# Reordering the start of a two-layer linear-attention and gated-MLP kernel: loads on one queue, LayerNorm on GpSimd, query weights transposed by DMA

## The chip, the cores and the metric

The kernel runs on one core of a Trainium2 chip. The metric is device time in microseconds (us) of one execution, median of several runs. The core's engines work side by side: TensorE (PE in the profile; PEld is its weight load), VectorE (DVE), ScalarE (ACT), GpSimd (POOL) and SyncE (SP), which here only issues DMAs. ScalarE can issue DMAs too.

## The reference

All tensors are bf16; S = 2048 tokens, D = 576 columns, H = 32 heads of 18 columns, F = 4608. Two layers, each an attention part A and a gated part B with the same weights in both layers:

```python
def _A_ref(x, wqkv, w_phi, wo):
    q, k, v = heads(x @ wqkv)
    pq = einsum("bhsd,hdf->bhsf", q, w_phi);  pk = einsum("bhsd,hdf->bhsf", k, w_phi)
    phi_q = concat([softmax(pq), softmax(-pq)]);  phi_k = concat([softmax(pk), softmax(-pk)])
    kv = einsum("bhsf,bhsd->bhfd", phi_k, v);  z = phi_k summed over s
    o = einsum("bhqf,bhfd->bhqd", phi_q, kv) / (einsum("bhqf,bhf->bhq", phi_q, z) + 1e-6)
    return merged(o) @ wo
def _B_ref(x, w_gate, w_up, w_down):
    return ((x @ w_gate) * (x @ w_up)) @ w_down

x = x + _A_ref(_layernorm(x), ...)
x = x + _B_ref(_layernorm(x), ...)
x = x + _A_ref(_layernorm(x), ...)
x = x + _B_ref(_layernorm(x), ...)
```

The LayerNorm has no weights. The attention is linear: `kv` and `z` need all tokens of the layer before any token's output can be formed.

## The kernel before

**Tiles.** The tokens are 16 tiles of 128, handled in 8 pairs. x stays in SBUF (`x_sb`). For each tile, LayerNorm statistics are made on VectorE (L1111, L1119), the logarithm and exponential that give 1/sqrt(variance) on ScalarE (L1132, L1134), and the normalised tile `xln` is written by one TENSOR_SCALAR (L1144). `xln` has 640 columns: its last 64 of 576 are repeated behind them, so that the two halves of TensorE's rows both have them after the transpose into `xT`. The transpose is TensorE's with a copy (L1152, L1155, the `fast` argument of `t_ln`, used where latency counts) or a DMA transpose issued by SP (L1159). For the plain pairs, `t_ln` writes 576 and 64 columns of each tile in two operations, both on GpSimd, or, for layer 1's attention (`boot`), both on GpSimd or VectorE as the planner prefers.

**Stages.** First come the loads (`t_load`: raw q and k weights `Wraw` in five slabs, x tiles, v weights), a test on the weights that writes `flag` (`t_flag`, L931 to L944), and the fusion of `w_phi` into the k and q weights (`t_fuse1`: a transpose of a slab into `WTk` or `WTq`, L1057 and L1060, then matmuls with a block-diagonal `BDphi`, L1071, and a cast, L1076). After the flag the program branches: with these inputs the branch without maxima (`fast=True`) runs. There, each tile gets a k and a v projection (L1185), four exponentials (`dd`, L1306), their sums (L1373, VectorE), reciprocals (L1376 on VectorE or L1380 on ScalarE), two products with them (L1388, GpSimd; VectorE for the last two tiles) and its key-value matmuls (L1427). When all 16 are through, `t_barrier` forms `BD` (L1518), tiles 0 and 1 are finished by `t_aout` (L1575 to L1639), normalised, and the gated part starts: L1715 (gate and up), L1762 and L1764 (product), L1789 and L1791 (down), pair by pair. The query projections of tiles 2 to 15 (`t_qproj`, L1330) fill TensorE meanwhile. Layer 1's gated part is interleaved with layer 2's key-value work (`k2`, `t_kv`) and with the attention outputs of later tiles. In `t_aout`, for tiles from 2 on, the last 64 columns of the attention output are repeated too, by a VectorE copy, before a DMA transpose.

**Memory that is shared in time.** `Wraw` and `WTk`, `WTq` lie where `Wg` and `Wu` (gate and up weights) are loaded later. So the last four of the eight loads of `Wg` and `Wu` wait for the fused q weights, and the first four for the last pair's `xT`.

**Order.** The program is written by a planner (`Sched`) when it is built. Each piece of work is a generator that yields operations with an estimated duration, the tiles read and written, and events. At each step the planner takes the waiting operation with the smallest key, its estimated start less several terms:

```python
key = (est - self.bias.get(int(th.prio), 0.0) - th.age - th.age0 - (self.hold if late else th.boost), -th.prio)
```

`age0` comes from the table `AGES` at the top of the file, in nanoseconds by the generator's name. An `alt` request names several engines and the planner takes the one that it expects to finish first. An operation with `port=True` on VectorE is planned not to overlap one on GpSimd. Every engine and queue then runs its list strictly in the planned order, with semaphore waits where a tile is produced elsewhere. Parameters in `K.__init__` steer the generators: `sload` and `aload` (early loads of SP's and ScalarE's queue), `lnb` (from which pair LayerNorm waits for the branch), `lnlead` and `vlead` (how far LayerNorm and v run ahead of key-value work), `qlead` (when the first query tiles start), `pqg` (when query projections may start), `fqp`, `fage2` (priorities), `wtdma` (which weights are transposed by DMA).

Of the kernel before, what the change touches and what calls it, by code (L numbers as in the profile page):

```python
# [8 lines left out]
ALU = mybir.AluOpType  # L9
# [7 lines left out]


AGES = {
    "ain1_0": 96, "ain1_1": 52, "ain1_11": -60, "ain1_12": -492, "ain1_13": 86, "ain1_14": -147, "ain1_5": -137, "ain1_6": -193, "ain1_9": -273,  # L20
    "ain2_14": -438, "ain2_15": -340, "aout1_0": -130, "aout1_1": -102, "aout1_2": -169, "aout1_3": -149, "aout2_0": -365, "aout2_1": 28,
    "aout2_2": -170, "aout2_3": -392, "bar1": -205, "bar2": 31, "bdphi": 104, "bepi0": -915, "bepi6": 256, "bepi7": -330, "flag": -70, "fusek0": -120,
    "fusek1": -40, "fusek2": 301, "fusek3": -147, "fuseq0": -35, "fuseq1": -124, "fuseq2": -148, "fuseq3": -151, "init": 401, "k2_6": -418,
    "k2ln0": 766, "k2ln1": 1415, "kv2_7": -134, "lnA1_0a": 245, "lnA1_0b": 360, "lnA1_2": 62, "lnA1_3": 52, "lnA1_4": -54, "lnB1_0a": -675,
    "lnB1_0b": -631, "lnB2_0a": -815, "lnB2_0b": -579, "pq1_10": -131, "pq1_11": 213, "pq1_2": 262, "pq1_3": -196, "pq1_4": -111, "pq1_5": 12,
    "pq1_6": 145, "pq1_9": 334, "pq2_11": 118, "pq2_12": 428, "pq2_15": 112, "pq2_2": 322, "pq2_3": 281, "pq2_4": 41, "pq2_5": 296, "pq2_6": -35,
    "pq2_8": -91, "v1_0": 39, "v1_1": -420, "v1_11": -111, "v1_13": -244, "v1_15": 580, "v1_2": -281, "v1_3": -122, "v1_5": -127, "v1_6": -124,
    "v1_8": -122, "v2_14": -755, "v2_15": -878,
}


# [265 lines left out]
class Sched:  # L297
# [110 lines left out]
    def run(self):  # L408
        tr = self.tr
        while True:  # L410
# [83 lines left out]
            for th in self.threads:  # L494
# [10 lines left out]
                elif r[0] == "pe2":  # L505
                    ops = r[1 + self.pe_mode]
                    est = max(self.free_at["pe"], self.ready(th, 10 + self.pe_mode, "pe", ops, True), th.t_ready)
                    th.alt = ("ops", "pe", ops, self.pe_mode)
                elif r[0] == "ops":
                    eng = r[1]  # L510
# [17 lines left out]
            if r[0] == "ops":  # L528
                eng = r[1]
                t = est  # L530
                first = True
                t_beg = t
                for o in r[2]:
                    deps = tr.deps_for(eng, o.reads, o.writes, o.excl, True, o.order)
                    if not first:
                        t = max(t, tr.ready_time(deps, eng))
                    if eng == "pe" and o.mode != self.pe_mode:
                        self.pe_mode = o.mode
                        if not first:
                            t += self.pe_switch  # L540
                    first = False
                    fin = t + o.dur
                    tr.record(eng, o.emit, o.reads, o.writes, o.excl, fin, deps)
                    self.busy[eng] += o.dur
                    t = fin
                    if eng == "pool" or o.port:
                        self.port[eng] = fin
                if self.log is not None:
                    self.log.append((th.name, eng, t_beg, t, len(r[2]), self.free_at[eng]))
                self.free_at[eng] = t  # L550
            else:
                _, group, emit, reads, writes, nbytes, dram_write = r[:7]
                immediate = r[7] if len(r) > 7 else False
                issue = est
                queue = r[9] if len(r) > 9 else "sp"
                if hasattr(self, "mark_time"):
                    start = max(issue, self.dma_free["sp"])
                    xfer = nbytes / self.dma_bw
                else:
                    start = max(issue + 1250.0, self.dma_free["sp"])  # L560
                    left, u = nbytes, start
                    for end, rate in ((3400.0, 290.0), (5000.0, 150.0), (1e9, 335.0)):
                        if u < end and left > 0:
                            d_ = min(left / rate, end - u)
                            left, u = left - d_ * rate, u + d_
                    xfer = u - start
                self.dma_free["sp"] = start + xfer
                sp_time = r[8] if len(r) > 8 else 480.0
                fin = max(start + xfer + (self.dma_lat if hasattr(self, "mark_time") else 600.0), issue + 2.1 * sp_time) + (1500.0 if sp_time > 1000 else 0.0)
                tr.record_dma(group, emit, reads, writes, fin, queue, dram_write, immediate)  # L570
                self.free_at[queue] = issue + sp_time
# [5 lines left out]
S, D, FF, H, DH = 2048, 576, 4608, 32, 18  # L577
# [58 lines left out]
class K:  # L636
    def __init__(self, nc, A_x, A_wqkv, A_w_phi, A_wo, B_w_gate, B_w_up, B_w_down, out, fast, base=None):
# [7 lines left out]
        self.XPS, self.XSM, self.XVX, self.NMX = (0, 6, 9, 0) if fast else (1, 4, 9, 2)  # L645
        self.BOUND = 40.0
        self.vrow = True
        self.vlead = 5
        self.row2 = True
        self.wtdma = ''  # L650
        self.valt = False
        self.qalt = True
        self.sload = [['x0', 0], ['raw', 0], ['x0', 1], ['raw', 2], ['raw', 3], ['raw', 4], ['wv', 0], ['x', 3]]
        self.aload = [['raw', 1], ['x', 1], ['x', 2]]
        self.rord = (0, 1, 2, 3, 4)
        self.fage = 300
        self.fageq = 0.0
        self.fage2 = 300
        self.lnb = 3
        self.pes = (0, 1, 2, 3, 4, 5, 6, 7, 8, 9, 10, 11, 12, 13)  # L660
        self.early = (2, 2)
        self.pex = 2
        self.qlead = 12 if fast else 8
        self.alt = 1.2
        self.wage = 10
        self.lnage = -3
        self.lnlead = 8
        self.pol0 = 1
        self.qdeep = (1, 1)
        self.urgent = 4  # L670
        self.pqp = (3, 3)
        self.pqg = 8 if fast else 10
        self.NPQ = 3
        self.NLAST = 3
        self.pqd = 100
# [1 line left out]
        self.qcrit = False  # L677
        self.fq = 3
        self.fqs = 2
        self.fqp = 6.5 if fast else 6.5  # L680
        self.sub2pool = False
        self.rboost = 500.0
        self.prio0 = (6, 7)
# [238 lines left out]
    def t_flag(self):  # L922
        s = self
        yield ("wait", "init")
        yield ("age", s.fage2)
        for kt in range(5):
            yield ("wait", ("ld", "raw", s.rord[kt]))
            if kt == 0:
                gots = yield ("acqn", ["pb"], 2)
                banks = [g_[1] for g_ in gots]  # L930
            yield ("ops", "pe", [Op(55, (lambda e, m=m, c0=c0, kt=s.rord[kt], bank=banks[m // 3], c=128 * (m % 3), st=(kt == 0 and c0 == 0 and m in (0, 3)), sp=(kt == 4 and c0 > 0): e.matmul(  # L931
                s.ps[:, bank, c:c + 128], s.Wraw[:, kt, c0 + 128 * m:c0 + 128 * m + 128], s.Wraw[:, kt, c0 + 128 * m:c0 + 128 * m + 128], start=st, stop=sp, skip_group_check=True)),
                reads=[("Wraw", s.rord[kt])], writes=[("pbd", banks[m // 3])], excl=[("pb", banks[m // 3])]) for c0 in (0, D) for m in range(5)])
        yield ("ops", "dve", [Op(d_dve(n), (lambda e, c=c, bank=bank, n=n: e.tensor_reduce(s.cst[:, c:c + 1], s.ps[:, bank, 0:n], AX.X, ALU.max)),
                                 reads=[("pbd", bank)], writes=[("cst", c)], excl=[("pb", bank)]) for c, bank, n in ((1, banks[0], 384), (2, banks[1], 256))])

# [150 lines left out]
    def t_ln(self, tiles, sig, fast=False, slot=None, banks=None):  # L1087
        s = self
# [47 lines left out]
        for j in js:  # L1136
# [4 lines left out]
                                                        bias=s.nmr[:, sl[j]:sl[j] + 1], scale=rstd[:, sl[j]:sl[j] + 1])),  # L1141
                      reads=xr + [("nmr", sl[j]), ("rstd", sl[j])], writes=[("xln", sl[j])]),
                   Op(240, (lambda e, j=j: e.copy(xln[:, sl[j], 576:640], xln[:, sl[j], 512:576])), reads=[("xln", sl[j])], writes=[("xln", sl[j])])]
            em = [(lambda e, j=j, a=a, b=b, c=c: e.tensor_scalar(xln[:, sl[j], a:b], x_sb[:, ss[j], c:c + b - a], s.nmean[:, sl[j]:sl[j] + 1], rstd[:, sl[j]:sl[j] + 1],  # L1144
                                                                 ALU.add, ALU.mult)) for a, b, c in ((0, 576, 0), (576, 640, 512))[:2 - fast]]
            yield ("alt", [(eng, [Op(d, em[i], reads=[("x", ss[j], 0), ("x", ss[j], 1), ("nmean", sl[j]), ("rstd", sl[j])], writes=[("xln", sl[j])], port=eng == "dve") for i, d in enumerate(dur)])
                           for eng, dur in (("pool", (790, 370)[:2 - fast]), ("dve", (400,) if fast else (400, 215)))[:1 + (fast or boot)]])
        for j in js:
            if fast:
                (_, bank), = yield ("acqn", ["pb"], 1)  # L1150
# [208 lines left out]
    def softmax_tail(self, sm, crit, pz=None, exps=True):  # L1359
# [25 lines left out]
        for br in range(2):  # L1385
            ev = dd[:, sm, :, br, :]
            rb = ss[:, sm, :].rearrange("p (g b) -> p g b", b=2)[:, :, br].unsqueeze(2).to_broadcast([128, H, DH])
            yield ("alt", [(eng, [Op(dur, (lambda e, ev=ev, rb=rb: e.tensor_tensor(ev, ev, rb, ALU.mult)),  # L1388
                                     reads=s.ddk(sm, br) + [("ss", sm)], writes=s.ddk(sm, br))])
                           for eng, dur in ((("pool", 1150), ("dve", 675))[crit > 1:1 + (crit > 1)] if s.fast else (("pool", 1150), ("dve", 675))[:1 + (crit > 1)])])  # L1390

    def t_v(self, L, st_):
# [134 lines left out]
    def t_aout(self, L, st_):  # L1527
# [69 lines left out]
            ops.append(Op(d_dve(288), (lambda e, i=i, ov=ov, rb=rb: e.tensor_tensor(ov, nv[i][:, :, 0:DH], rb, ALU.mult)),  # L1597
                          reads=[("pbd", banks[i])] + denk, writes=[okeys[i]] + okeys[2:], excl=[("pb", banks[i])]))
        if st_ >= 2:
            ops.append(Op(130, (lambda e: e.tensor_copy(o[:, 576:640], o[:, 512:576])), reads=okeys, writes=okeys))  # L1600
        yield ("ops", "dve", ops)
        yield ("rel", "o", ob)
        for bank in banks:
            yield ("rel", "pb", bank)
# [475 lines left out]
```

## Time and profile before

| | us |
|---|---|
| median of 9 runs | 1076.73 |
| lowest, highest | 1074.65, 1080.02 |
| the profiled execution's own time | 1076.34 |
| its span, first to last instruction | 1074.6 |
| first gated-unit matmul of layer 1 (L1715) | 101.9 |
| first gated-unit matmul of layer 2 | 619.5 |

How to read the profile: "L1144" is a line of the kernel; a group row gives the line, engine, operation, `out<-in` tiles and shapes, the count, then busy us and mean ns of one, then the engine's idle time before it and what ended it. "SPq" and "ACTq" are DMA issues. A busy PE is one with matmuls in its pipeline, not one at full rate. The granted TensorE clock was 0.998 of full speed over the span.

### The profile page before, as it was taken

How to read it: one execution, taken by the hardware profiler on the slowest of the kernel's cores; microseconds unless marked ns; L12 is line 12 of the kernel's file. 1: busy time of each engine (PE TensorE's matmuls, PEld its weight loads, DVE VectorE, ACT ScalarE, POOL GpSimd, SP SyncE). 2: the span in 40 equal slices, each digit the busy share in tenths (PEclk: the TensorE clock that was granted, in tenths of full speed). 3: DMA queues.
4: the chain of work that ended last, by engine and by line, in shares of the span. 5: the costliest groups of instructions: out<-in, count | busy, mean ns of one | idle time of the engine just before them, and what ended most of it. 6: DMA issues, size and time to landing. Idle time of an engine off the chain costs nothing.

```text
span 1074.6 us, 34340 instructions
## 1 busy us (share of the span) xinstructions
PE 1051.1 (98%) x15766; PEld 804.2 (75%) x15828; DVE 484.0 (45%) x982; ACT 346.6 (32%) x839; POOL 196.2 (18%) x226
## 2 busy tenths in 40 slices
PE   7989999999999999999999999999999999999997
PEld 5657868778686878878686786777778686868683
DVE  6976526354443535425232754434434243424131
ACT  5777214324141422314141742231313131302030
POOL 2753004022230403103020030201010101000000
PEclk9999999999999999999999999999999999999999
DMA  5496265260927246182605134636282808081704
GB/s 168 85 292 209 42 180 93 80 168 21 226 28 201 60 117 140 35 195 37 199 15 167 34 59 122 137 86 173 60 199 36 222 16 241 16 223 15 210 2 146
DMA packets 177626, 127.79 MB, mean 119 GB/s; under 512 B 96576, under 2 KB 175680, under 8 KB 176320
## 3 DMA queue, kind: packets, MB, share of 16 engines
q1 hardware_dynamic: 176176, 124.57, 45.2%
q8 instruction: 126, 2.06, 0.8%
q10 hardware_dynamic: 1296, 0.92, 0.3%
q14 instruction: 28, 0.23, 0.1%
HBM read 100.82 MB, written 2.36 MB: 96 GB/s over the span
## 4 chain that ended last, share of the span: by engine, by line
PE 92%; DVE 2%; DMA 2%; ACT 2%; issue 1%
PE ps L1715 53%; PE ps L1789 20%; PE ps L1185 11%; PE ps L1791 4%; PE ps L1575 1%; DVE xln L1144 1%; DVE ss_w4f L1373 1%; DMA wdr<-in_B_w_down_dram 1%; DMA wdx<-in_B_w_down_dram 1%; PE ps L1427 1%; ACT dd_h1g L1306 1%; PE ps L1173 0%; PE ps L1152 0%; DMA wst<-in_A_w_phi_dram 0%; ACT dd_w3f L1306 0%
## 5 line engine op out<-in xcount | busy, mean ns | idle before, releaser
L1715 PE MATMUL ps<-xT,Wg 64*128 64x256 bf16 x4608 | 581.9, 269 | 0.0
L1715 PE MATMUL ps<-xT,Wu 64*128 64x256 bf16 x4608 | 581.1, 269 | 0.0
L1715 PEld LDWEIGHTS ps<-xT,Wg 64*128 64x128 bf16 x4608 | 430.6, 94 | 29.1 <-issue 3.1
L1715 PEld LDWEIGHTS ps<-xT,Wu 64*128 64x128 bf16 x4608 | 431.8, 94 | 27.3
L1764 DVE TENSOR_TENSOR hT<-ps,hT 128x512 bf16<-128x512 f32 x288 | 199.1, 691 | 303.9 <-ACT hT L1762 303.9
L1762 ACT CAST hT<-ps 128x512 bf16<-128x512 f32 x288 | 168.4, 585 | 413.6 <-PE ps L1715 406.6
L1789 PE MATMUL ps<-wdr,hT 128*128 128x512 bf16 x922 | 237.9, 380 | 0.7 <-DMA wdr<-in_B_w_down_dram 0.6
L1388 POOL TENSOR_TENSOR dd<-dd,ss 128x576 bf16<-128x576 bf16 x92 | 106.6, 1185 | 490.2 <-ACT ss L1384 490.1
L1791 PE MATMUL ps<-wdr,hT 128*128 128x64 bf16 x960 | 184.9, 193 | 2.3 <-issue 0.5
L1789 PEld LDWEIGHTS ps<-wdr,hT 128*128 128x128 bf16 x960 | 93.8, 98 | 112.0 <-DMA wdr<-in_B_w_down_dram 1.6
L1715 PE MATMUL ps<-xT,Wr 64*128 64x256 bf16 x1152 | 168.3, 269 | 0.0
L1832 DVE TENSOR_TENSOR x_sb<-ps,x_sb 128x64 bf16<-128x64 f32 x32 | 7.0, 219 | 225.8 <-PE ps L1791 225.8
L1144 POOL TENSOR_SCALAR xln<-x_sb,nmean,rstd 128x576 bf16<-128x576 bf16 x86 | 51.7, 607 | 254.4 <-DVE nmean L1125 173.6
L1791 PEld LDWEIGHTS ps<-wdr,hT 128*128 128x128 bf16 x960 | 94.1, 98 | 0.2
L1384 ACT ACTIVATE ss<-ss 128x64 f32<-128x64 f32 x92 | 23.5, 258 | 178.6 <-DVE ss L1373 177.7
L1373 DVE TENSOR_REDUCE ss<-dd 128x64 f32<-128x1152 bf16 x48 | 63.5, 1345 | 20.0 <-ACT dd L1306 18.9
L1715 PEld LDWEIGHTS ps<-xT,Wr 64*128 64x128 bf16 x1152 | 65.1, 94 | 6.3
L1185 PE MATMUL ps<-Wk,xT 64*128 64x288 bf16 x576 | 49.0, 284 | 2.8 <-ACT Wq L1076 1.7
L1185 PE MATMUL ps<-Wv,xT 64*128 64x288 bf16 x576 | 49.8, 283 | 1.6 <-ACT eT L1551 0.5
L1789 PE MATMUL ps<-wdx,hT 128*128 128x512 bf16 x168 | 50.4, 380 | 0.4 <-DMA wdx<-in_B_w_down_dram 0.3
L1111 DVE BATCH_NORM_STATS2 st<-x_sb 128x6 f32<-128x288 bf16 x120 | 46.2, 444 | 1.4 <-DMA x_sb<-in_A_x_dram 1.3
L1185 PE MATMUL ps<-Wq,xT 64*128 64x288 bf16 x576 | 41.1, 283 | 0.6 <-ACT dd_w3f L1306 0.4
(125 smaller groups left out, 740.9 us busy)
## 6 DMA issues: line engine op xcount, KB each, us to landing
wdr<-in_B_w_down_dram SPq DMA_DIRECT2D x240, 288.0 KB, 3.5
wdx<-in_B_w_down_dram SPq DMA_DIRECT2D x48, 288.0 KB, 3.5
Wg<-in_B_w_gate_dram SPq DMA_DIRECT2D x4, 1152.0 KB, 13.8
Wu<-in_B_w_up_dram SPq DMA_DIRECT2D x4, 1152.0 KB, 15.6
out_dram<-x_sb SPq DMA_DIRECT2D x16, 144.0 KB, 2.5
x_sb<-in_A_x_dram SPq DMA_DIRECT2D x5, 288.0 KB, 3.7
Wraw<-in_A_wqkv_dram SPq DMA_DIRECT2D x4, 304.0 KB, 6.2
xT<-xln SPq DMA_TRANSPOSE x54, 2.5
```

Of the source, the lines that this page charges most:

```text
L1111: ops.append(Op(d_dve(288), (lambda e, j=j, h=h, src=src: e.bn_stats(st[:, sl[j], 6 * h:6 * h + 6], src)), reads=rd, writes=[("st", sl[j], ...
L1144: em = [(lambda e, j=j, a=a, b=b, c=c: e.tensor_scalar(xln[:, sl[j], a:b], x_sb[:, ss[j], c:c + b - a], s.nmean[:, sl[j]:sl[j] + 1], rstd[ ...
L1185: out.append(Op(61, (lambda e, h=h, k=k, st=(i == 0 and k == 0), sp=(i == 1 and k == 3): e.matmul(s.ps[:, banks[h], 0:N], L[r, k, :], Wm[r ...
L1306: yield ("ops", "act", [Op(d_actc(288), (lambda e, br=br, h=h, bank=bank: e.activation(s.dd[:, sm, 16 * h:16 * h + 16, br, :], s.ps[:, ban ...
L1373: Op(1265, (lambda e: e.tensor_reduce(ss[:, sm, :], e4, AX.X, ALU.add)), reads=s.ddk(sm, 0) + s.ddk(sm, 1), writes=[("ss", sm)]),
L1384: yield ("ops", "act", [Op(200, (lambda e, kw=kw: e.activation(ss[:, sm, :], ss[:, sm, :], **kw)), reads=[("ss", sm)], writes=[("ss", sm)])])
L1388: yield ("alt", [(eng, [Op(dur, (lambda e, ev=ev, rb=rb: e.tensor_tensor(ev, ev, rb, ALU.mult)), reads=s.ddk(sm, br) + [("ss", sm)], write ...
L1715: out.append(Op(54.3, (lambda e, bank=bank, cs=cs, lhsT=lhsT, rhs=rhs, st=st, sp=sp: e.matmul(ps[:, bank, cs].rearrange("p (a n) -> p a n" ...
L1762: yield ("ops", "act", [Op(480, (lambda e, gb=gb, p=p: e.copy(hT[:, p, :], ps[:, gb, :])), reads=[("gu", gb)], writes=[("hT", p)] + (s.raw ...
L1764: yield ("ops", "dve", [Op(600, (lambda e, ub=ub, p=p: e.tensor_tensor(hT[:, p, :], ps[:, ub, :], hT[:, p, :], ALU.mult)), reads=[("gu", u ...
L1789: ops = [Op(d_pe(512), (lambda e: e.matmul(s.ps[:, bank, 0:512], lhsT, s.wslot(slot)[:, fi, 0:512], start=(f == 0), stop=(f == NF - 1))), ...
L1791: Op(d_pe(64) + 3, (lambda e: e.matmul(s.ps[:, z, 64 * sl:64 * sl + 64], lhsT, s.wslot(slot)[:, fi, 512:576], start=(f == 0 and (sl == 0 o ...
```

## The change

- `AGES` is replaced by another table, and these parameters get other values: `vlead` 5 to 7, `lnb` 3 to 5, `lnlead` 8 to 7, `qlead` 12 to 14, `pqg` 8 to 10, `fqp` 6.5 to 6.15, `fage2` 300 to 600 (all for the branch that runs, or both). The planner's estimate of the early DMA rate is 350 instead of 335 bytes per ns.
- All early loads but `w_phi` go to SP's queue, raw weight slabs 1 and 2 first; `t_flag` takes the slabs in the order of loading.
- The q weights are transposed by DMA from SP (`wtdma = 'q'`), not by TensorE with a copy.
- Plain pairs are normalised on GpSimd alone (`lndve = False`), one operation of 576 columns for each tile, and the repeat of the last 64 columns is one operation for both tiles, on GpSimd or ScalarE.
- The VectorE alternative of the softmax products is marked `port`; the repeat of the attention output's last columns is planned as an operation of its own, marked `port`.

```diff
@@ Sched.run
-                    for end, rate in ((3400.0, 290.0), (5000.0, 150.0), (1e9, 335.0)):
+                    for end, rate in ((3400.0, 290.0), (5000.0, 150.0), (1e9, 350.0)):
@@ K.__init__
-        self.vlead = 5
+        self.vlead = 7
-        self.wtdma = ''
+        self.lndve = False
+        self.wtdma = 'q'
-        self.sload = [['x0', 0], ['raw', 0], ['x0', 1], ['raw', 2], ['raw', 3], ['raw', 4], ['wv', 0], ['x', 3]]
-        self.aload = [['raw', 1], ['x', 1], ['x', 2]]
-        self.rord = (0, 1, 2, 3, 4)
+        self.sload = [['raw', 1], ['raw', 2], ['x0', 0], ['x0', 1], ['raw', 3], ['raw', 0], ['raw', 4], ['wv', 0], ['x', 1], ['x', 2], ['x', 3]]
+        self.aload = []
-        self.fage2 = 300
-        self.lnb = 3
+        self.fage2 = 600
+        self.lnb = 5
-        self.qlead = 12 if fast else 8
+        self.qlead = 14 if fast else 8
-        self.lnlead = 8
+        self.lnlead = 7
-        self.pqg = 8 if fast else 10
+        self.pqg = 10 if fast else 10
-        self.fqp = 6.5 if fast else 6.5
+        self.fqp = 6.15 if fast else 6.5
@@ t_flag
+        rord = [k_[1] for k_ in s.sload if k_[0] == "raw"]
...
@@ t_ln
-            em = [(lambda e, j=j, a=a, b=b, c=c: e.tensor_scalar(xln[:, sl[j], a:b], x_sb[:, ss[j], c:c + b - a], s.nmean[:, sl[j]:sl[j] + 1], rstd[:, sl[j]:sl[j] + 1],
-                                                                 ALU.add, ALU.mult)) for a, b, c in ((0, 576, 0), (576, 640, 512))[:2 - fast]]
...
+            em = (lambda e, j=j: e.tensor_scalar(xln[:, sl[j], 0:576], x_sb[:, ss[j], :], s.nmean[:, sl[j]:sl[j] + 1], rstd[:, sl[j]:sl[j] + 1], ALU.add, ALU.mult))
...
+                           for eng, dur in (("pool", 790), ("dve", 400))[:1 + (fast or (boot and s.lndve))]])
+        if not fast:
+            xo, xi = xln[:, s0:s1, 576:640], xln[:, s0:s1, 512:576]
+            yield ("alt", [(eng, [Op(dur, em, reads=key("xln"), writes=key("xln"))]) for eng, dur, em in (
+                ("pool", 420, lambda e: e.tensor_copy(xo, xi)), ("act", 210, lambda e: e.copy(xo, xi)))])
@@ softmax_tail
-                                     reads=s.ddk(sm, br) + [("ss", sm)], writes=s.ddk(sm, br))])
+                                     reads=s.ddk(sm, br) + [("ss", sm)], writes=s.ddk(sm, br), port=eng == "dve")])
@@ t_aout
-            ops.append(Op(130, (lambda e: e.tensor_copy(o[:, 576:640], o[:, 512:576])), reads=okeys, writes=okeys))
-        yield ("ops", "dve", ops)
+            ops.append(Op(100, (lambda e: e.tensor_copy(o[:, 576:640], o[:, 512:576])), reads=okeys, writes=okeys, port=True))
+        yield ("ops", "dve", ops[:2])
+        if st_ >= 2:
+            yield ("ops", "dve", ops[2:])
```

## The prediction

> **What bounds the kernel now.** I read the page first. TensorE is busy nearly all of the span, the other engines less than half of it.
>
> ```profile
> PE 1051.1 (98%) x15766; PEld 804.2 (75%) x15828; DVE 484.0 (45%) x982; ACT 346.6 (32%) x839; POOL 196.2 (18%) x226
> ```
>
> That average hides stages, so the second view is the windows table, cut where the timeline shows the first gated-unit matmul (101.9 us), the end of layer 1's last down-projection (584) and the first gated-unit matmul of layer 2 (619.5). Columns: length, busy time of PE, PEld, DVE, ACT, POOL (instructions), granted clock, DMA share, GB/s.
>
> ```profile
> 0.00:20.00 20.00, 14.07 (x160) 10.58 (x162) 12.57 (x42) 9.32 (x23) 5.39 (x20) 1.00 0.58 187
> 20.00:60.00 40.00, 37.15 (x538) 25.54 (x534) 37.30 (x73) 31.57 (x111) 22.57 (x21) 1.00 0.47 98
> 60.00:80.00 20.00, 17.28 (x240) 11.07 (x242) 13.90 (x15) 15.51 (x49) 13.55 (x12) 1.00 1.07 335
> 80.00:102.00 22.00, 21.97 (x322) 15.56 (x319) 14.06 (x30) 16.18 (x40) 4.75 (x4) 1.00 0.65 251
> 102.00:584.00 482.00, 479.93 (x7352) 376.15 (x7378) 210.15 (x426) 146.57 (x350) 100.83 (x114) 1.00 0.45 109
> 584.00:619.50 35.50, 35.21 (x472) 23.73 (x472) 23.73 (x51) 20.90 (x60) 0.32 (x1) 1.00 0.26 78
> 619.50:1074.60 455.10, 445.50 (x6698) 341.53 (x6728) 172.31 (x349) 106.56 (x209) 48.84 (x56) 0.99 0.46 116
> ```
>
> The two long rows, 937 us, are TensorE at full rate and the other engines idle over half the time: nothing in this change removes matmuls there. The first 102 us are another matter. Between 20 and 60 us VectorE is busy 37.3 of 40. PE's 37.15 there is not 37 us of work: in the chain, 64 back-to-back projection matmuls take 4.23 us, 0.066 each, and counting the stretch's matmuls so (the other kinds by their own closest spacing in the trace) gives about 33 us of work in 40, and 14.7 in the 20 after. So the first stage is where time can come from.
>
> The third view is the chain of waits in that stage (start, length, what). It hangs on VectorE almost without a break from 41.2 to 63.4 us; its last part:
>
> ```profile
> 59.00 0.35 DVE xln L1144
> 59.37 1.64 DVE xln L1144 x2
> 61.03 1.04 DVE xln L1144
> 62.08 1.27 DVE ss_w4f L1373
> 63.91 1.21 ACT dd L1306 x4
> ```
>
> The LayerNorm application of a pair of tokens (L1144) stands on the chain and a softmax sum waits behind it. Three such pairs are there (from 41.21, 51.27 and 59.00 us), 9.2 us of the chain with the small breaks. The timeline says why a pair costs 3.2:
>
> ```profile
> 29.73 0.76 DVE L1144 TENSOR_SCALAR xln<-x_sb,nmean,rstd 128x576 bf16<-128x576 bf16 x2
> ...
> 51.27 3.16 DVE L1144 TENSOR_SCALAR xln<-x_sb,nmean,rstd 128x576 bf16<-128x576 bf16 x4
> 52.01 2.39 POOL L1388 TENSOR_TENSOR dd_h1g<-dd_h1g,ss_w4f 128x576 bf16<-128x576 bf16 x2 [0.69 <-ACT ss_w4f L1380]
> ```
>
> One tile (its 576 columns and the repeat of 64) takes 0.76 us alone, so two would take 1.52; beside GpSimd's softmax products two take 3.16. VectorE pays, GpSimd does not (2.39 for two, elsewhere 2.33).
>
> **The change part by part.**
>
> *Token LayerNorm to GpSimd.* Group rows of the first stage:
>
> ```profile
> L1144 DVE TENSOR_SCALAR xln<-x_sb,nmean,rstd 128x576 bf16<-128x576 bf16 (+1 forms) x24 | 13.5, 584 | 0.7 <-ACT rstd L1134 0.3
> ...
> L1144 POOL TENSOR_SCALAR xln<-x_sb,nmean,rstd 128x576 bf16<-128x576 bf16 x1 | 0.8, 824 | 0.0
> L1144 POOL TENSOR_SCALAR xln<-x_sb,nmean,rstd 128x64 bf16<-128x64 bf16 x1 | 0.4, 393 | 0.1
> ```
>
> Of the 24, two belong to pair 1, which may stay on VectorE (0.84 us). So VectorE sheds 12.6 us: eleven tiles. GpSimd takes 11 x 0.82 = 9.0 us, plus six joint repeats of 128 columns, each between ScalarE's smallest operations (about 0.2) and twice GpSimd's 0.39, on either engine: 1 to 5 us. Its busy time from 20 to 80 us is 36.1 of 60 and becomes 46 to 50. On the chain the gain is at most the 9.2 us. VectorE's 37.3 falls to 24.7 of 40, so next is ScalarE, 31.6 of 40, which leaves 8.4 at most. Against it: a pair now takes 2 x 0.82 + 0.39 = 2.0 us on an in-order GpSimd, behind up to 2.4 us of products, and both transposes wait for the joint repeat, where the first tile's could start after 0.76. Queued behind each LayerNorm on GpSimd are products that TensorE's key-value matmuls wait for. Lower end: 9 to 14 us more on GpSimd with none of its idle time (14 of the 50 us from 25 to 75) filled: a loss of 6. I take a gain of 4.0: half of what ScalarE leaves. What is late next is the exponentials.
>
> A rule that speaks against this part: the Trainium skill, GPSIMD Engine Reference, section 4.1, keeps elementwise work on VectorE. Alone, 0.82 against 0.42 us agrees, and by that rule alone the move would cost about 12 x 0.4 = 5 us; the contended 3.16 per pair against 2.0 says otherwise.
>
> *Query weights by DMA.* Off TensorE go 25 transposes, five groups of 0.45 us (row below) and a change of matmul mode before most, 2.3 to 3.5 us; off ScalarE two copies of 0.73, off VectorE three of 0.48. On the chain of this stage only the copies stand, 0.60, 0.40 and 0.40.
>
> ```profile
> 55.12 0.45 PE L1057 MATMUL ps<-ident,Wraw 128*128 128x128 bf16 x5
> ...
> xT<-xln SPq DMA_TRANSPOSE x54, 2.5
> ```
>
> Added are five SP transposes of the same 128x640 form, issue 1.23 us each, landing after 2.4 to 6.5. They wait only for weights loaded long before, so they block SP for 6 us in all, spread over five fusions; behind them stand token transposes and x loads. The weights were ready at 60.9 and gate the last four gate and up loads (issued from 67.0). These landed by 90.6, 11 us before use: that cover hides a delay; if it went, each us late would be a us. Bounds: gain 2.3, loss 2.5 (two token transposes held once each). I take a gain of 1.0.
>
> *Early loads on one queue.* Slabs of 304 KB land about 1.13 us apart (8.01, 9.14). The last raw weights landed at 10.28 with 288 KB of x ahead of them that now come later: about 1.0 us earlier. Token tile 0 lands later than its 2.99, but its LayerNorm application started only at 5.70. SP now issues the two x pairs that ScalarE's queue issued, at 0.4 to 0.7 us each, before its own last one. Bounds: 1.5 either way. I take a gain of 0.5.
>
> *Order, port flags, split repeat of attention columns, earlier query tiles.* No instruction is added. In the long stages LayerNorm pairs have one operation fewer on a GpSimd busy 21% and 11% there: nothing, hidden by TensorE. In the stage 584 to 619.5 TensorE's work, counted as above, is 33.6 of 35.5, so 2 either way; I take 0.
>
> Sum against the profiled execution, 1076.34 (span 1074.6 and 1.7 around it): 1076.34 - 4.0 - 1.0 - 0.5 = 1070.8. The median of the runs, 1076.73, is 0.4 above, so 1071.2.
>
> **The rivals.**
>
> 1. *GpSimd becomes the bound of 20 to 80 us* (slower). For it: its 46 to 50 us of work must run in order between the first products (24.9) and the last key-value matmul, and products and LayerNorm wait for each other's results; its idle time there was waits for reciprocal sums from ScalarE and VectorE. Against: those came late because VectorE was full. It decides when GpSimd still idles over about 5 of the 50 us. Then the stage ends about 6 us later than now: 1082.5.
>
> 2. *ScalarE's limit is reached* (faster still). The whole 8.4 us, and 1.5 from weights and loads: 1076.7 - 9.9 = 1066.8. Against: of ScalarE's waits between 15 and 102 us, 6.5 us ended with VectorE's sums and over 10 with TensorE's results, and only the first kind goes away.
>
> 3. *Hidden anyway.* Query projections fill TensorE from 78 us on; if the tail from the last key-value matmul (85.4) to 101.9 keeps its place because the gate and up loads (25 us from their start) or another order hold it, the gain is under 2 us: 1076.
>
> **How the numbers follow.** My case 0.52, rival 2 0.10, rival 3 0.10, rival 1 0.20, and 0.08 for a new order that loses over 2 us elsewhere. Two tenths of a per cent, 2.15 us, is about what can be told from no change. Faster 0.62, same 0.10, slower 0.28. The range reaches from a little below rival 2 to just short of rival 1's price: 1065.5 to 1081.5. The forecast's own range is 1066.5 to 1074.5.
>
> **What would show it.** Right: no L1144 of two-tile pairs on VectorE before 102 us; VectorE near 25 of 40 busy from 20 to 60; the chain there on ScalarE and TensorE; the first gated-unit matmul at 95 to 98 us, not 101.9; the rows after it as long as now. Wrong: GpSimd busy 4.8 of every 5 us with products waiting behind LayerNorm; xT transposes landing over 5 us after issue; a first gated-unit matmul after 104; or the same start and a longer 584 to 619.5 stage.

## The result, and the profile after

The changed kernel takes 1080.15 us (median of 13 runs, 1078.08 to 1082.57); the kernel before, measured beside it, 1076.92. The ratio is 1.0033, with a 95% interval of [1.0024, 1.0041]: slower, by 3.5 us. The profiled execution took 1080.04 (span 1078.3).

The windows table of the changed kernel, cut as before (length, busy PE, PEld, DVE, ACT, POOL, granted clock, DMA share, GB/s):

```profile
20.00:60.00 40.00, 37.25 (x572) 26.78 (x568) 27.49 (x49) 34.39 (x122) 35.69 (x36) 1.00 0.61 115
60.00:80.00 20.00, 18.12 (x275) 12.93 (x277) 14.95 (x17) 14.88 (x45) 11.69 (x10) 1.00 1.04 365
80.00:102.00 22.00, 16.47 (x240) 12.10 (x236) 11.10 (x29) 11.77 (x29) 1.65 (x2) 1.00 0.57 213
102.00:584.00 482.00, 478.28 (x7295) 375.04 (x7326) 216.01 (x427) 148.47 (x354) 92.36 (x93) 0.99 0.42 107
```

From 20 to 60 us VectorE fell from 37.30 busy of 40 to 27.49, and TensorE got 34 more matmuls through. GpSimd rose from 22.57 to 35.69. From 80 to 102 us TensorE lost what it had won: 240 matmuls in place of 322. The chain of waits from 40 to 62 us stands on GpSimd where it stood on VectorE:

```profile
44.89 3.46 POOL dd_h1g L1393 x3
48.36 1.61 POOL xln L1146 x2
49.96 5.72 POOL dd_h1g L1393 x5
55.68 1.14 POOL dd_w3f L1393
56.83 1.62 POOL xln L1146 x2
58.44 0.02 issue
58.46 0.30 ACT xln L1152
```

A pair's LayerNorm takes 1.61 there, where it took 3.16 on VectorE, but products (L1393) now stand ahead of it and behind it. The same chain later:

```profile
74.43 3.61 PE ps L1190 x53
78.04 0.61 PE ps L1550 x9
78.65 10.22 PE ps L1190 x162
88.87 1.20 PE ps L1432 x30
90.06 1.00 DVE BD L1523 x2
...
101.81 1.04 DVE xln L1146
102.85 0.05 issue
102.90 0.90 PE ps L1157 x6
```

And the timeline around it (start, length, engine, line, `out<-in`, the idle time before it and what ended it):

```profile
77.90 0.75 DVE L1393 TENSOR_TENSOR dd_h1g<-dd_h1g,ss_w4f 128x576 bf16<-128x576 bf16 x1
...
88.80 0.86 PE L1432 MATMUL ps<-vx_h2g,dd_h1g 128*128 128x76 bf16 x18
...
102.90 0.85 PE L1157 MATMUL ps<-ident,xln 128*128 128x128 bf16 x6 [3.22 <-DVE xln L1146]
...
104.37 0.39 PE L1722 MATMUL ps<-xT,Wg 64*128 64x256 bf16 x1 [0.62 <-DVE xT L1160]
```

The last softmax product ends at 78.65; before, it ended at 84.19. So the first stage did get shorter, by 5.5 us. But on TensorE's list about 160 query-projection matmuls (L1190) stand between it and the last key-value matmuls (L1432): 10.2 us, in which nothing is waited for. Then comes the tail, from those matmuls over `BD`, the finishing of tiles 0 and 1 and their LayerNorm to the first gated-unit matmul (L1722). It is one long dependence over three engines (TensorE, VectorE, ScalarE), 15.6 us from 88.80, and no query projection is left to fill TensorE in it. Windows of the changed kernel's tail and of its first gated-unit matmuls:

```profile
90.00:104.40 14.40, 7.35 (x79) 4.64 (x77) 10.23 (x26) 6.39 (x16) 2.33 (x2) 0.93 0.42 131
...
99.00:102.40 3.40, 0.57 (x6) 0.34 (x6) 2.22 (x7) 1.70 (x6) 2.05 (x2) 0.99 0.00 0
...
104.40:109.20 4.80, 4.80 (x46) 3.46 (x48) 1.17 (x1) 0.51 (x2) 2.33 (x2) 0.50 0.22 40
109.20:114.00 4.80, 4.80 (x92) 4.20 (x88) 2.64 (x3) 2.87 (x6) 0.00 (x0) 1.00 0.33 65
```

The same tail of the kernel before:

```profile
86.90:101.90 15.00, 14.97 (x204) 10.48 (x206) 10.84 (x26) 11.76 (x30) 2.42 (x2) 1.00 0.48 172
```

There TensorE was busy all 15 us, with 204 matmuls. The chain of the kernel before shows what filled it: query projections (L1185) between the transposes (L1152) of tiles 0 and 1 and up to the first gated-unit matmul:

```profile
94.72 2.92 PE ps L1185 x46
97.64 0.51 PE ps L1152 x6
98.14 0.60 PE ps L1185 x8
98.74 0.51 PE ps L1152 x6
99.25 2.80 PE ps L1185 x44
```

In the changed kernel it is busy half the time, with a gap of 3.2 us at 99.7, and after it the granted clock is 0.50, half clock from here on, from 102.4 to 109.2: 46 gated-unit matmuls in 4.8 us where the next 4.8 us hold 92, so about 2.4 us lost.

The sum of the difference: first gated-unit matmul 104.37 against 101.89, +2.5; half clock, +2.4; 36 more query-projection matmuls done before it (252 against 216, at 0.066), -2.4. That is 2.5 of the 3.7 us between the spans; 1.2 lies after it and was not traced further.

### The profile page after: what moved, and what is told of

The parts are those of the page before. It is cut to its first block, busy times and chain, and to the rows that moved or that the text cites. A ratio compares the mean times of both kernels' runs of the same rounds, so it can differ in the third digit from the quotient of the medians.

```text
span 1078.3 us, 34256 instructions
## 1 busy us (share of the span) xinstructions
PE 1048.0 (97%) x15741; PEld 804.8 (75%) x15803; DVE 480.5 (45%) x962; ACT 348.3 (32%) x841; POOL 194.2 (18%) x210
## 4 chain that ended last, share of the span: by engine, by line
PE 92%; DMA 3%; ACT 1%; POOL 1%; DVE 1%; issue 1%; ACTq 0%
PE ps L1722 52%; PE ps L1796 21%; PE ps L1190 12%; PE ps L1798 4%; PE ps L1580 1%; POOL dd_h1g L1393 1%; DMA wdx<-in_B_w_down_dram 1%; PE ps L1432 1%; DMA xT<-xln 1%; DMA oT<-dd 1%; DMA wdr<-in_B_w_down_dram 0%; ACT dd_h1g L1311 0%; PE ps L1157 0%; PE ps L933 0%; PE ps L1178 0%
## 5 line engine op out<-in xcount | busy, mean ns | idle before, releaser
L1722 PE MATMUL ps<-xT,Wg 64*128 64x256 bf16 x4608 | 583.8, 270 | 0.8 <-DVE xT L1160 0.6
L1722 PE MATMUL ps<-xT,Wu 64*128 64x256 bf16 x4608 | 582.9, 270 | 0.0
L1722 PEld LDWEIGHTS ps<-xT,Wg 64*128 64x128 bf16 x4608 | 431.3, 94 | 31.8 <-issue 3.3
L1722 PEld LDWEIGHTS ps<-xT,Wu 64*128 64x128 bf16 x4608 | 432.6, 94 | 26.4
L1393 POOL TENSOR_TENSOR dd<-dd,ss 128x576 bf16<-128x576 bf16 x92 | 107.1, 1190 | 459.5 <-ACT ss L1389 459.5
L1722 PE MATMUL ps<-xT,Wr 64*128 64x256 bf16 x1152 | 170.1, 270 | 0.0
L1146 POOL TENSOR_SCALAR xln<-x_sb,nmean,rstd 128x576 bf16<-128x576 bf16 x56 | 45.4, 820 | 314.7 <-ACT rstd L1136 198.5
L1722 PEld LDWEIGHTS ps<-xT,Wr 64*128 64x128 bf16 x1152 | 66.4, 94 | 6.5
L1190 PE MATMUL ps<-Wk,xT 64*128 64x288 bf16 x576 | 48.0, 283 | 3.5 <-ACT xT L1160 1.7
L1190 PE MATMUL ps<-Wv,xT 64*128 64x288 bf16 x576 | 49.2, 283 | 0.5 <-ACT vx_w0g L1422 0.2
L1190 PE MATMUL ps<-Wq,xT 64*128 64x288 bf16 x576 | 40.6, 283 | 0.6 <-ACT eT L1556 0.3
```

Of the source, the lines that this page charges most:

```text
L1146: em = (lambda e, j=j: e.tensor_scalar(xln[:, sl[j], 0:576], x_sb[:, ss[j], :], s.nmean[:, sl[j]:sl[j] + 1], rstd[:, sl[j]:sl[j] + 1], ALU ...
L1190: out.append(Op(61, (lambda e, h=h, k=k, st=(i == 0 and k == 0), sp=(i == 1 and k == 3): e.matmul(s.ps[:, banks[h], 0:N], L[r, k, :], Wm[r ...
L1722: out.append(Op(54.3, (lambda e, bank=bank, cs=cs, lhsT=lhsT, rhs=rhs, st=st, sp=sp: e.matmul(ps[:, bank, cs].rearrange("p (a n) -> p a n" ...
```

## The experiments

The theory: *the list*. The stage became shorter as forecast, and the gain is lost because the new list of TensorE puts the query projections ahead of the last key-value matmuls and leaves the tail empty. The first rival: *the engine*. GpSimd is the new bound, and the loss is the LayerNorm's. The second: *the clock*. The half clock alone makes the loss. Later runs put the parts of the change on and off. Ratios are to the kernel before, run beside it on the same chip, with 95% intervals; "product" is the end of the last softmax product, "key-value" the start of the last key-value matmul, "first G" the first gated-unit matmul, "q" the query-projection matmuls of tiles 2 to 15 (252 in all) that started before first G, all from the traces.

| run | median us | ratio | product | key-value | first G | q |
|---|---|---|---|---|---|---|
| before | 1076.92 | | 84.2 | 86.1 | 101.9 | 216 |
| after | 1080.15 | 1.0033 [1.0024, 1.0041] | 78.6 | 90.1 | 104.4 | 252 |
| e1_kv_first | 1072.59 | 0.9953 [0.9936, 0.9970] | 78.4 | 78.9 | 98.0 | 226 |
| e9_no_q_ages | 1073.42 | 0.9960 [0.9944, 0.9975] | 79.5 | 80.9 | 96.4 | 198 |
| e3_before_q_first | 1087.84 | 1.0102 [1.0085, 1.0119] | 83.2 | 96.2 | 111.1 | 252 |
| e10_before_kv_first | 1077.76 | 1.0004 [0.9990, 1.0018] | 84.2 | 84.9 | 99.9 | 162 |
| e2_fill_tail | 1077.77 | 1.0004 [0.9990, 1.0017] | 79.8 | 91.3 | 105.3 | 252 |
| e4_before_ln_gpsimd | 1076.57 | 0.9998 [0.9987, 1.0009] | 84.9 | 86.9 | 104.2 | 252 |
| e5_ln_twice | 1077.92 | 1.0005 [0.9994, 1.0017] | 85.2 | 85.8 | 104.9 | 226 |
| e6_kvfirst_wq_on_pe | 1078.10 | 1.0007 [0.9995, 1.0020] | 84.9 | 85.5 | 105.1 | 234 |
| e7_kvfirst_old_loads | 1077.97 | 1.0006 [0.9996, 1.0016] | 84.2 | 85.4 | 101.8 | 190 |
| e8_before_new_loads | 1079.29 | 1.0020 [1.0011, 1.0030] | 89.5 | 91.7 | 107.0 | 244 |
| e11_before_wq_dma | 1074.70 | 0.9979 [0.9964, 0.9994] | 81.3 | 82.0 | 99.0 | 198 |
| e13_before_ln_and_wq | 1074.47 | 0.9987 [0.9978, 0.9996] | 83.1 | 88.2 | 103.2 | 252 |
| e12_new_table | 1067.13 | 0.9918 [0.9905, 0.9932] | 76.1 | 77.6 | 96.1 | 244 |

### The place of the last key-value matmuls

`e1_kv_first` is the changed kernel with one edit in `t_ain`, the generator of a tile's key-value work. An age is subtracted from the key, so the key-value matmuls of tiles 12 to 15 go earlier in the list:

```diff
         sm0, vx0 = s.sm_of[st_ - 1], s.vx_of[(1, st_ - 1)]
+        if st_ >= 12:
+            yield ("age", 900.0)
```

> The changed kernel, but from token tile 12 on the key-value matmuls get an age of 900 ns, so that the planner puts them on TensorE as soon as their inputs are there and not behind the query projections. Theory 1 (order on TensorE): in the changed kernel the last key-value inputs were ready at 78.65 us, but 162 query projection matmuls (10.2 us) stood ahead of the last key-value matmuls (88.8), so the tail to the first gated-unit matmul (104.4) had nothing to fill TensorE with. Here the last key-value matmuls are at 79 to 80 us, query projections fill the tail, the first gated-unit matmul comes at 95 to 98 us with no stretch at half clock behind it, and the time is 1069 to 1073 us. Theory 2 (GpSimd is the bound since LayerNorm went there): the chain up to 78 us and its length stay, moving the key-value matmuls wins nothing that the tail does not take back: first gated-unit matmul at 102 or later, 1079 to 1080 us.

Measured: 0.9953, against 1.0033 for the changed kernel, so 0.8% or 8.6 us by the ratios for an edit that adds no instruction (the medians differ by 7.6 us, the two profiled spans by 6.6). Its timeline, and its windows from the last key-value matmuls to the first gated-unit matmul and over the 4.8 us after:

```profile
78.42 0.69 PE L1432 MATMUL ps<-vx_h2g,dd_h1g 128*128 128x76 bf16 x13 [0.16 <-DVE dd_h1g L1393]
79.05 1.54 PE L1190 MATMUL ps<-Wq,xT 64*128 64x288 bf16 x18
```

```profile
79.80:98.00 18.20, 17.07 (x231) 12.02 (x231) 11.70 (x29) 11.99 (x31) 1.98 (x2) 1.00 0.67 265
98.00:102.80 4.80, 4.80 (x92) 4.14 (x90) 2.37 (x3) 3.60 (x10) 2.67 (x3) 1.00 0.34 65
```

The key-value matmuls now wait for the product itself (DVE, 0.16 us), and the last of them starts 11.2 us earlier; the query projections lie behind them, in the tail. From that matmul to first G it is 19.1 us instead of 14.2, but nearly full, and the half clock does not come. In the two profiled executions the sum is: first G 6.3 us earlier, 26 projections put off behind it (-1.7), half clock gone (+2.4), 7.0 us against the 6.6 between the spans. GpSimd is as full as in the changed kernel (35.53 of 40 from 20 to 60 us), so the loss is not GpSimd's.

`e9_no_q_ages` asks what in the change makes that order. It is the changed kernel without ten entries of the new `AGES`, those of the query projections of layer 1:

```diff
-    "m2": 138, "pq1_10": 275, "pq1_11": 592, "pq1_2": -268, "pq1_4": -125, ..., "pq1_8": 701, "pq1_9": 258,
+    "m2": 138,
```

> The changed kernel without the ten entries of its table of ages that belong to layer 1's query projections (pq1_2 to pq1_11, up to 701 ns ahead); everything else as changed. Theory A (these entries put the query projections ahead of the last key-value matmuls): the last key-value matmuls follow the last softmax product within 2 us, the first gated-unit matmul comes at 97 to 100 us, no half clock in that tail, 1071 to 1075 us. Theory B (the gates decide, pqg and qlead, or the 100 ns that the planner adds for a change of matmul mode): the query projections stay ahead, last key-value matmul at 88 us or later, 1079 us or more.

Measured: 0.9960, the gain of `e1_kv_first` within the noise. So the order comes from those entries.

`e3_before_q_first` makes the fault alone: the kernel before, with the age of the last key-value matmuls (the same line) at -3000.

> The kernel before, whole, but from token tile 12 on its key-value matmuls get an age of minus 3000 ns, so that the planner puts all query projections of layer 1 ahead of the last key-value matmuls, as in the changed kernel. LayerNorm, loads and query weights as before the change. Theory 1: this alone makes the loss: tail without fill, first gated-unit matmul at 104 to 109 us instead of 101.9, half clock behind it, 1080 to 1086 us. Theory 2: without LayerNorm on GpSimd there is no loss: 1076 to 1078 us.

Measured: 1.0102, about 11 us slower with no instruction added. Its chain and the tail's window:

```profile
81.98 12.26 PE ps L1185 x195
94.24 0.05 issue
94.29 0.66 PE ps L1185 x8
94.95 1.20 PE ps L1427 x30
```

```profile
98.00:111.00 13.00, 6.89 (x50) 4.05 (x48) 10.79 (x22) 6.98 (x20) 4.01 (x4) 0.83 0.43 132
```

The same picture as in the changed kernel: 203 projections ahead of the key-value matmuls, a half-empty tail, and half clock in two stretches (99.7 to 103.1, 109.9 to 116.7).

`e10_before_kv_first` is the kernel before with the edit of `e1_kv_first`.

> The kernel before with the age of 900 ns for the last key-value matmuls, the edit of e1, alone. Theory A (what e1 won is the loss of the changed order and its earlier last product): in the kernel before only 17 query projection matmuls, 1.1 us, stood between the last product (84.2) and the last key-value matmuls (86.1), so first gated-unit matmul at 100 to 102 us and 1074.5 to 1077.5 us. Theory B (the edit is a gain of its own, in any order): 1073 us or less.

Measured: no difference, though first G came 2.0 us earlier. 54 fewer query-projection matmuls were done before it, 3.6 us that come later. So first G is not a measure by itself: it must be read together with the work that was put off. In the kernel before this part of the list had nothing to give; the fault came with the new table.

### The empty tail and the clock

`e2_fill_tail` leaves the order of the changed kernel and adds matmuls whose results are not used, 512 columns each, from the last key-value matmuls to the end of tile 1's LayerNorm:

```diff
+    def t_fill(self):
...
+        yield ("wait", ("num", 1, 0))
+        (_, bank), = yield ("acqn", ["pb"], 1)
+        yield ("age", 250.0)
...
+            yield ("ops", "pe", [Op(216, (lambda e: e.matmul(s.ps[:, bank, 0:512], s.ident[:], s.Wk[:, 0, 0:512], ...)), ...)])
...
```

> The changed kernel in its own order, with 19 matmuls added (512 columns each, into a PSUM bank that is free, result unused) on TensorE in the gaps of the tail between the last key-value matmuls and the first gated-unit matmul. They do no useful work. Theory 1, as far as the clock goes: the gaps (the longest 3.2 us, 99.7 to 102.9) were followed by 6.8 us at half the clock (102.3 to 109.2), which cost 2.4 to 3.4 us; with the gaps filled the first gated-unit matmul stays at 104 to 105 us, there is no half clock there, and the time falls to 1077 to 1078. Theory 2: the half clock is a by-product of no weight, 1080 or more.

Measured: 1.0004 against 1.0033, with first G 0.9 us later and no half clock anywhere before 120 us. So the clock is worth about 3 us (3.1 by the ratios; 2.4 by the count of matmuls above) of the 7 to 9 that the order costs; the rest is the tail's place. The clock theory accounts for part of the loss, and is itself a consequence of the empty tail.

### LayerNorm on GpSimd

`e4_before_ln_gpsimd` is the kernel before with this part alone: `t_ln` as in the change and `lndve = False`.

> The kernel before with the LayerNorm part alone: plain pairs on GpSimd only, one joint repeat of the last columns for a pair. Order table, loads and query weights as before. Theory 1: the part itself is no loss; the last softmax product before the key-value matmuls comes 2 to 6 us earlier than 84.2 us, and the time is 1072 to 1077 us. Theory 2: GpSimd is busy over 34 of the 40 us from 20 to 60, the last product is no earlier than 84 us, and the time is 1078 to 1081 us.

Measured: 0.9998 [0.9987, 1.0009]: nothing. (First G is 2.3 us later, but 36 more projections, 2.4 us, were done before it.) From 20 to 60 us VectorE was relieved (29.84 of 40 in place of 37.30) and GpSimd filled (36.36 in place of 22.57):

```profile
20.00:60.00 40.00, 37.96 (x566) 26.96 (x562) 29.84 (x54) 34.20 (x121) 36.36 (x37) 1.00 0.48 89
```

The chain shows where the earlier start went:

```profile
58.57 9.22 DMA xT<-xln
```

The last pair's transposes were issued 1.1 us earlier than in the kernel before (58.6 against 59.7), but landed 8.3 and 9.2 us after issue instead of 4.7 and 6.5. The last of two large loads into `Wr` that SP issues ahead of them went out 0.6 us before them; in the kernel before it was 3.4 us. TensorE idled 2.2 us for them. In both kernels the first of the pair landed about 2 us after that load did (67.8 after 65.7, and 66.2 after 64.2). That the loads hold them up is argued from this and from the order on the queue; it was not tried by moving the loads.

`e5_ln_twice` doubles the suspected cost in the mended kernel: GpSimd writes the plain pairs of layer 1's attention twice, once into an unused tile.

```diff
...
+            one = (lambda e, j=j: e.tensor_scalar(xln[:, sl[j], 0:576], ...))
+            junk = (lambda e, j=j: e.tensor_scalar(s.junk[:, ss[j] % 3, :], ...))
+            em = (lambda e, one=one, junk=junk: (junk(e), one(e))[1]) if boot else one
```

> The kernel of e1 (key-value matmuls first) in the same planned order, but each LayerNorm application of layer 1's plain pairs is done twice on GpSimd, the first time into a buffer that nothing reads: 12 more operations of 0.82 us, 9.8 us, on an engine that is busy 35.5 of the 40 us from 20 to 60. Theory A (GpSimd has become the bound of that stretch): the last softmax product moves from 78.4 to 84 us or later and the first gated-unit matmul from 98.0 to 102 or later, 1077 to 1082 us. Theory B (the stretch is bound by the order and by TensorE or ScalarE, GpSimd has room): the first gated-unit matmul moves by less than 2 us, 1072 to 1074.5 us.

Measured: 1.0005 against 0.9953 for `e1_kv_first`: 5.6 us by the ratios, and the last product 6.9 us later (3.4 us of half clock from 47.9 on included), for twelve added operations of 0.824, 9.9 us in all:

```profile
L1148 POOL TENSOR_SCALAR junk<-x_sb,nmean,rstd 128x576 bf16<-128x576 bf16 x12 | 9.9, 824 | 5.1 <-ACT rstd L1137 5.1
```

So GpSimd's list is on the path of 20 to 60 us in this order: about two thirds of what is put on it reaches the last product. Each added operation also stands ahead of the real one, so the run does not separate GpSimd's load from a later LayerNorm.

### Query weights and loads

`e11_before_wq_dma` is the kernel before with `wtdma = 'q'` and nothing else.

> The kernel before with the query weights transposed by DMA alone. Theory A (about 1 us, as its rows say): last softmax product 82 to 84.2 us, 1075 to 1077 us. Theory B (the old table of ages does not fit it): last product later than 85 us, first gated-unit matmul at 104 us or later, 1078 us or more.

Measured: 0.9979 [0.9964, 0.9994], 2.3 us faster by the ratio, with an interval of 0.6 to 3.9; the last product comes 2.9 us earlier. VectorE falls to 33.94 busy of 40 with most of the LayerNorm still on it:

```profile
20.00:60.00 40.00, 35.13 (x503) 23.14 (x505) 33.94 (x68) 29.93 (x108) 24.40 (x24) 1.00 0.57 104
```

`e13_before_ln_and_wq` adds the LayerNorm part to that.

> The kernel before with two parts of the change, LayerNorm of plain pairs on GpSimd and query weights by DMA; table of ages, parameters and loads as before. The DMA part alone gave 1074.7 us with the last softmax product at 81.3. Theory A (LayerNorm on GpSimd wins once TensorE and the copies are relieved): last product at 79 us or earlier, 1071 to 1074 us. Theory B (LayerNorm on GpSimd only moves the bound from VectorE to GpSimd): last product at 81 us or later, 1074 to 1077.5 us.

Measured: 0.9987 [0.9978, 0.9996]: no better than the query weights alone. The last product comes 1.8 us later than with them alone. Besides, 70 projections, 4.4 us, stand ahead of the last key-value matmuls here, a part of the fault of the order, so this run does not price the LayerNorm by itself.

`e6_kvfirst_wq_on_pe` is `e1_kv_first` with `wtdma = ''`, and `e7_kvfirst_old_loads` is `e1_kv_first` with the old `sload`, `aload` and `rord`.

> The kernel of e1 with the query weights transposed on TensorE again, as before the change. Theory A (each part is worth about what its rows say, 1 us here): last softmax product 79 to 80 us, first gated-unit matmul 98.5 to 100, 1073 to 1075 us. Theory B (the table of ages fits this set of parts alone, and taking a part out spoils the order): last product 82 us or later, first gated-unit matmul 101 or later, 1076 to 1082 us.

> The kernel of e1 with the early loads on two queues in their old order. Theory A (the part is worth about 0.5 us): branch 0.5 to 1 us later, last softmax product 78.5 to 80 us, first gated-unit matmul 98 to 100, 1072 to 1075 us. Theory B (fitted table): last product 82 us or later, 1076 to 1082 us.

Measured: 1.0007 and 1.0006, so each part taken out costs 0.5%, the whole gain of `e1_kv_first`. How much of that is the part, and how much the other order that the planner writes without it, these runs do not separate; in the first the clock was halved from 35.3 to 42.1 us, in the second from 19.3 and from 50.0 for 3.4 us each.

`e8_before_new_loads` is the kernel before with the new load order.

> The kernel before with the new order of early loads on one queue alone. Theory A: the branch comes 0.5 to 1.5 us earlier, the time is 1075 to 1077 us. Theory B (its own table of ages fits its own loads): the order of the first stage changes, with more query projections ahead of the last key-value matmuls, first gated-unit matmul at 104 us or later, 1078 to 1084 us.

Measured: 1.0020 [1.0011, 1.0030]. The branch after the flag came 1.4 us earlier (16.85 against 18.22), and the last product 5.3 us later. The planner wrote another list, with ages that were found for the old loads. TensorE stood half idle from 21.9 us, and the clock was halved for 10.2 us:

```profile
21.90:25.30 3.40, 1.76 (x26) 1.09 (x24) 3.37 (x7) 2.79 (x8) 1.05 (x1) 1.00 0.39 88
25.30:35.50 10.20, 8.07 (x78) 6.01 (x77) 7.28 (x21) 5.11 (x15) 3.60 (x4) 0.50 0.36 92
```

### A version that beats both

`e12_new_table` is `e1_kv_first` with `AGES` searched again for that kernel, and nothing else.

> The kernel of e1 (all parts of the change, key-value matmuls first) with a table of ages searched anew for this set of parts; nothing else differs. Theory A (the parts leave room that the order uses): the last key-value matmuls within 2 us of the last softmax product, at least 160 query projection matmuls behind them, first gated-unit matmul at 94 to 98 us, no half clock before it, 1067 to 1072 us. Theory B (e1's gain is a chance of one order): 1074 us or more.

Measured: 1067.13 us, 0.9918 [0.9905, 0.9932]: 8.7 us faster than the kernel before and, by the ratios, 12 faster than the change. Its windows:

```profile
20.00:60.00 40.00, 37.02 (x561) 26.50 (x560) 28.59 (x54) 34.27 (x121) 34.51 (x35) 1.00 0.65 118
60.00:80.00 20.00, 19.83 (x328) 14.68 (x326) 15.47 (x17) 15.20 (x47) 13.40 (x11) 1.00 1.03 385
80.00:102.00 22.00, 21.78 (x321) 16.80 (x319) 12.71 (x30) 15.29 (x39) 5.44 (x5) 1.00 0.56 203
```

GpSimd is nearly as full as in the changed kernel from 20 to 60; what differs is TensorE from 60 on: 328 and 321 matmuls, where the change has 275 and 240. Against `e1_kv_first` the profiled span is 6.0 us shorter: first G comes 1.9 earlier with 18 more projections (1.2) done, and the other 2.9 lie after first G, where the new table differs too. No table was searched again for the kernel before, so how much of the 8.7 us the search alone would give it is not shown.

## Why the prediction was wrong

**The step that failed: the order, and the tail with it.** The forecast gave the new order and the earlier query tiles a price of 0, because no instruction is added, and carried 5.5 us of gain in the first stage through to the end. The stage did give 5.5 us at the last product (84.19 to 78.65). That this equals the sum of 4.0, 1.0 and 0.5 is luck: alone, the three parts moved the last product by +0.7, -2.9 and +5.3 us (`e4_before_ln_gpsimd`, `e11_before_wq_dma`, `e8_before_new_loads`). The order then cost 7 to 9 us (`e1_kv_first`): key-value matmuls 10.2 us behind their operands, a tail with nothing to fill it, and about 3 us of half clock (`e2_fill_tail`). Without it the time is 1072.6 and the first gated-unit matmul at 98.0, the forecast's end of 95 to 98. The fact needed was in the profile before: 21.97 of 22.00 busy from 80 to 102, in a tail that is one dependence chain, with projections at each of its waits (the lines at 94.72 to 99.25 above), says that TensorE is full there only because projections are held back for it. Rival 3 came near: it named these projections, and another order that could hold the tail, but priced that at a gain under 2 us and not at a loss. The case of a new order that loses elsewhere had 0.08; its price was set at over 2 us, without a mechanism.

**LayerNorm to GpSimd: wrong in what comes next.** VectorE went to 27.49 of 40, where 24.7 was forecast (the row of 24 operations ran to 62 us, and 2.1 of its 13.5 us lie past 60), and a pair took 1.62, and 1.93 to the end of its repeat on ScalarE, near the 2.0. GpSimd's busy time from 20 to 80 us became 47.4, inside the 46 to 50. But the gain of 4.0 rested on ScalarE being the next limit; GpSimd's list was on the path (`e5_ln_twice`), 35.69 of 40, with ScalarE at 34.39. Alone the part gave 0 (`e4_before_ln_gpsimd`, -1.4 to +1.0 us), and no gain showed on top of the query weights (`e13_before_ln_and_wq`). Rival 1 named this mechanism; its price, a stage 6 us later than now, did not come. The Trainium skill, GPSIMD Engine Reference, section 4.1, keeps elementwise work on VectorE. By the times alone (0.82 against 0.42 us a tile) the move would cost about 5 us, an estimate, and by the contended pairs (3.16 against 2.0) it gains; the measurement lies between, at nothing.

**Query weights by DMA: right in sign.** Forecast 1.0, measured 2.3 us with an interval of 0.6 to 3.9 (`e11_before_wq_dma`), so the forecast lies inside it. Three of the five copies that left stood on the chain, as the prediction says; besides, with that part in, the planner put three more LayerNorm operations on GpSimd, so that VectorE keeps 21 in the first stage, 9.3 us, in place of 24 and 13.5. A part of the LayerNorm's move is thus inside this gain. The five transposes landed 2.5 to 4.7 us after issue there and 2.5 to 5.1 in the changed kernel; what queueing on SP cost was not measured apart.

**Early loads: right at the start only.** Alone they brought the last raw weights 2.0 us earlier (8.30 against 10.28), where 1.0 was forecast, and the branch 1.4. In the changed kernel, with its other parameters, the branch came 2.9 us earlier. What that was worth depended on the list: alone a loss of 0.2% (`e8_before_new_loads`), while taking them out of the new one loses 0.5% (`e7_kvfirst_old_loads`).

**Beyond the sum.** Alone the three parts change the time by 0, -0.2% and +0.2%, in the right order together by -0.5%; taking the query weights or the loads out again costs all of it, and the LayerNorm part was not taken out. A sum of parts is therefore not the price of a list that was searched with all of them. How much of each single run is the part and how much a list that no longer fits it stays open: every edit changes what the planner writes after it.

## What to carry to other kernels

On an engine that runs its list in order, independent work is free only where the engine would wait: look up what stands between the last operand's arrival and the matmul that needs it, and keep the filler for the dependence chain behind it. A stage that gets shorter gives nothing until the first instruction of the next stage moves, and that start must be read together with the work put off beyond it. When a new order comes with a change, price the order as a part of its own, with a range as wide as the stage that it rearranges.

## What the runs showed of the hardware

In the first 120 us half clock came in stretches of 3.4, 6.8 or 10.2 us, each after 3.4 us in which TensorE had matmuls for only 0.6 (the changed kernel) to 2.1 us (`e7_kvfirst_old_loads`, before 19.3). The changed kernel had a gap of 3.2 us, which agrees with the Trainium skill, TensorE: Matmul & The Clock Gate, section "Why this matters for your kernels", that asks for no idle gap over about 3 us. But a gap is not needed: in `e8_before_new_loads` the stretch before had matmuls for 1.76 of 3.40 us and no gap over 2 us, and so had `e6_kvfirst_wq_on_pe` (1.77):

```profile
31.90:35.30 3.40, 1.77 (x30) 1.44 (x30) 3.17 (x10) 1.92 (x8) 3.40 (x4) 0.99 0.43 96
```

The kernel before had 1.66 of 3.40 from 57.0 to 60.4 and kept full clock, so a low share does not always bring it; what else decides is not shown.

A token transpose, 2.5 us from issue to landing in the median of the kernel before, took up to 6.5 there, where SP had issued the last load into `Wr` 3.4 us ahead of it, up to 5.8 in the changed kernel, where it was 3.2 us, and 7.5 and 9.2 in `e11_before_wq_dma` and `e4_before_ln_gpsimd`, where that was 0.6 us. In all four kernels it landed 0.5 to 2.1 us after that load did. So the landing, and not only the issue of about 1.2 us, has to be priced when a transpose stands behind loads; that the loads are the cause was not tried.
